# Two edits in a staged attention kernel: a two-slot gate on weight conversions, and a third key tile joined on POOL

## The chip, the cores and the metric

One Trainium2 chip, one core. The metric is the device time of one launch in microseconds, median of three runs; lower is better.

## The reference

Three blocks follow each other. The first is attention in which a query sees only keys that share its nearest centroid; the second mixes tokens through cosine and sine of a projection; the third is a low-rank token mixer and a feed-forward layer.

```python
# q, k, v: (2, 8, 768, 64); 16 centroids for each head
mask   = q_assign[:, :, :, None] == k_assign[:, :, None, :]
scores = where(mask, scale * q @ k.T, -1e9)
attn   = exp(scores - max(scores)); attn /= sum(attn) + 1e-9
x      = attn @ v                              # -> (2, 768, 512)
theta  = x @ w_theta
y      = w_tok_r @ (x * cos(theta)) + w_tok_i @ (x * sin(theta))
u      = x + y;   u = u + relu(u @ w_ch)
h      = (u.T @ U @ V).T + u
out    = h + relu(h @ w_ch1) @ w_ch2
```

The weight inputs are float64 in memory, except q, k, v and the centroids. The kernel loads their 8-byte words and makes float32 of them on the chip.

## The kernel before

Attention runs in eight groups g (0 to 7), each one batch and two heads h. Keys are cut into six tiles kt of 128. P, the exponentials of the scores, is kept transposed: `pt[g, h, kt]` has keys on partitions and 768 queries on the free axis. A group is walked in six slots p (0 to 5). In one slot TensorE makes the scores of two key tiles of one head (`scores_pair`, L304; ACT takes the exponentials, L309) and the plain maxima of the next group's scores (`max_pair`, L251; VectorE reduces them, L255). `max_split` (L271 and L272, POOL) splits the maxima in two bf16 parts after slots 2 and 5, and `max_rows` (L282, L285) puts them as rows into the packed queries. PSUM is a ring of eight banks, given out in order.

In slot 5 of groups 1 to 6 TensorE then multiplies P with v (`pv`, L317) and adds up P over the keys with a matrix of ones (`sum_keys`, L346): one round of four matmuls (8 records in the trace) for each key tile that is handed to it. `join_keys` (L332) adds key tiles 0 and 1 of a head beforehand, in slots 1 and 4, on POOL in groups 0 to 3 and on VectorE after that, so five rounds are left. VectorE transposes the result (L349); in slot 2 of the following group `row_sums` (L358, L359, then eight small copies on POOL, L365) takes the reciprocal, and in slot 5 `spread` (L371) and `norm_x` (L375) scale the group's x.

Splitting and packing of group g + 2 happens in slots 0 and 1 (`split_hi` L188 on ACT, `split_lo` L193 on POOL, then 16 transfers by `pack` through L213), masks of group g + 2 in slot 2 or 3 (`mask_rows`, ACT and 8 transfers through L213). SyncE issues all transfers, in order.

Conversions of weights fill gaps. A `Convert` loads its tile into one of three staging buffers (`load`, L390), then ACT takes the high words (`magnitude`, L399), VectorE shifts the low words (`low`, L402) and joins both (`join`, L406); then ACT rounds a high part (`wh`, L411) and POOL subtracts it (`wl`, L415). Each call of `conv_step` does one of these: `magnitude` (unless done before), `low`, nothing, then a last step that joins, puts the following tile's `magnitude` on ACT, and issues the next load. `wh` and `wl` of a finished tile come at the next slot's start, or at the end of a group. While attention runs, `held[0]` is true.

Which work falls into a slot is counted out by `fill(t)`: the slot's allowance t is added to a debt `owed`, and items are taken until it is not above zero, first from the list `bg` (the cluster assignment of a later group, L128 to L152, `spread`, `norm_x`, each with a price), then conversion steps at 1.0. The allowance is 0.3 in most slots, 9.6 in slot 5 (4.8 in groups 0 and 1). Weights come in the order wth 0 to 2 (queued at group 1), wr 0, wi 0, wr 1, wi 1, wr 2, wi 2 (group 2), and the other six, `late`, at group 6.

The mixer follows (`theta` L534, `ymix` L576 and so on); it asks for each converted tile by `conv_until`.

Of the kernel before, what the change touches and what calls it, by code (L numbers as in the profile page):

```python
# [16 lines left out]
ALU = mybir.AluOpType  # L17
# [8 lines left out]
NT = S // P  # L26
# [15 lines left out]
def tile_cluster_block(ctx: ExitStack, tc: tile.TileContext, qk, v, cent, wth, wr, wi, wch,  # L42
                       u_in, v_in, w1, w2, cst, out):
    nc = tc.nc
# [7 lines left out]
    def slot(name, dt=F32, shape=None):  # L52
        return sp.tile(shape or [P, S], dt, tag="slot", name=name)
# [5 lines left out]
    def bank(name, keep=None):  # L59
        i = ring.popleft()  # L60
        if keep is None:
            ring.append(i)
        else:
            kept.setdefault(keep, []).append(i)
        return pp.tile([P, 512], F32, tag=f"bank{i}", name=name)
# [46 lines left out]
    def cols(hf):  # L112
        return slice(hf * HALF, (hf + 1) * HALF)
# [174 lines left out]
    pt, v_t, pvt, xT = {}, {}, {}, {}  # L288
# [24 lines left out]
    def pv(g, kt, hf):  # L313
        if kt == 0 and hf == 0:
            pvt[g] = banks("pv", "pv")
        for r in range(0, P, 32):
            nc.tensor.matmul(out=pvt[g][hf][r:r + 32, :HALF], lhsT=v_t[g][:, kt, r:r + 32],  # L317
                             rhs=pt[g, r // 64, kt][:, cols(hf)],
                             start=(kt == 0), stop=(kt == NT - 1))
# [7 lines left out]
    rl, lsum, joined = {}, {}, {}  # L327

    def join_keys(g, h, eng):
# [2 lines left out]
        eng.tensor_tensor(t, pt[g, h, 0], pt[g, h, 1], op=ALU.add)  # L332
        joined[g, h] = t

    def sum_keys(g, a, n=3):

        ps = bank("l")
        x = [[pt[g, h, kt] for kt in range(3 * a, 3 * a + n)] for h in range(2)]
        if (g, 1) in joined and a == 0:
            x = [[joined.pop((g, h)), *x[h][2:]] for h in range(2)]  # L340
        n = len(x[0])
        for i in range(n):
            for h in range(2):
                for hf in range(2):
                    o = 32 * (2 * h + hf)
                    nc.tensor.matmul(out=ps[o:o + 32, :HALF], lhsT=ones, rhs=x[h][i][:, cols(hf)],  # L346
                                     start=(i == 0), stop=(i == n - 1))
        lt = slot("lt")[:, :HALF]
        nc.vector.transpose(lt, ps[:, :HALF])  # L349
        lsum[g, a] = lt  # L350
# [67 lines left out]

    conv_load, conv_in, conv_do, conv_after = deque(), deque(), deque(), deque()
    held = [False]  # L420

    def conv_start():
        while conv_load and len(conv_in) < STAGED:
            c = conv_load.popleft()
            c.load()
            conv_in.append(c)

    def conv_step(n=1):

        for _ in range(n):  # L430
            if conv_after and not held[0]:
                conv_after.popleft()()
            if not conv_do:
                conv_start()
                if not conv_in:
                    return
                c = conv_in[0]

                def last(c=c):
                    c.join()  # L440
                    conv_in.popleft()
                    conv_after.extend([lambda f=f: f(c) for f in c.done])
                    if conv_in:
                        conv_in[0].magnitude()
                    conv_start()

                conv_do.extend((c.low, lambda: None, last))
                if c.t is None:
                    conv_do.appendleft(c.magnitude)
            conv_do.popleft()()  # L450
# [6 lines left out]
    def weigh_in(src, n, dst):  # L457
        return [Convert(src, n, i, keep_split(dst)) for i in range((n + S - 1) // S)]
# [384 lines left out]
    def attention():  # L843


        ORDER = [(0, 0), (0, 2), (0, 4), (1, 0), (1, 2), (1, 4)]
        BURST = (2, 5)
        pvq = deque()
        held[0] = True

        def next_pv():
            g, kt, hf = pvq.popleft()
            pv(g, kt, hf)
            if kt == NT - 1 and hf:
                pv_out(g)

        for g in range(NG):
            nxt = g + 1 < NG
            if g == 1:
                conv_load.extend(weigh_in(wth, NP * DM, wth_t))  # L860
                conv_start()
            if nxt:
                load_v(g + 1)
            if g < 2:
                bg.extend(assign.pop(g + 2))
            if g + 3 < NG:
                for i in range(2):
                    load_raw(g + 3, i)
            if g == 2:
                tok = [c for p in zip(weigh_in(wr, NT * S, wr_t), weigh_in(wi, NT * S, wi_t)) for c in p]  # L870
                conv_load.extend(tok[:6])
                conv_start()
                late = tok[6:]
            if g == 6:
                conv_load.extend(late)
                conv_start()
            if not nxt:
                for t in range(NP):
                    bg.append((1., lambda t=t: split_x(0, t, nc.gpsimd)))
            order = [(1, 0), None, (1, 2), None, (1, 4), None] if g == 0 else ORDER  # L880
            for p in range(NT):
                ready = len(pvq)
                if order[p]:
                    h, a = order[p]
                    scores_pair(g, h, a)
                    if h:
                        pvq.extend((g, kt, hf) for kt in (a, a + 1) for hf in range(2))
                if g == 0 and p < 2:
                    mask_direct(1, p, nc.scalar if p else nc.vector)
                if nxt:  # L890
                    max_pair(g + 1, p // 3, 2 * p % 6)
                    if p % 3 == 2:
                        max_join(g + 1, p // 3)

                while conv_after:
                    conv_after.popleft()()
                if p in ((1, 4) if g < 4 or not nxt else (2, 4)):
                    join_keys(g, p // 4, nc.gpsimd if g < 4 else nc.vector)
                    if 4 <= g < NG - 1 and p == 4:
                        owed[0] -= .95  # L900
                if p < 2 and g + 2 < NG:
                    split_half(g + 2, p)
                if p == (3 if g < 2 else 2) and g + 2 < NG:
                    mask_rows(g + 2)
                long = 0 < g < NG - 1 and p == 5
                if long:
                    if g + 3 < NG:
                        (_, sims), *items = assign_items(g + 3)
                        sims()
                        bg.extend(items)  # L910
                    max_rows(g + 1, 0)
                if g > 0 and p == 5:
                    bg.appendleft((.95, lambda: norm_x(g - 1)))
                    bg.appendleft((.97, lambda: spread(g - 1)))
                fill(2.5 if not nxt else .3 if p not in BURST or (g > 1 and p == 2) else 9.6 if g > 1 else 4.8)
                if not nxt:
                    for _ in range(min(ready, (2, 2, 2, 0, 4, 4)[p])):
                        next_pv()
                    if p == 5:
                        sum_keys(g, 0)  # L920
                elif long:
                    ready = len(pvq) - (6 if g == NG - 2 else 0)
                    for n in range(ready):
                        if n == ready // 2:
                            max_rows(g + 1, 1)
                        next_pv()
                    sum_keys(g, 0, NT)
                elif p == 2 and g < 2:
                    if g > 0:
                        max_rows(g, 1)  # L930
                        sum_keys(g - 1, 1)
                    for _ in range(min(ready, 6)):
                        next_pv()
                elif p == 5:
                    max_rows(g + 1, 0)
                    for _ in range(min(ready, 6)):
                        next_pv()
                    sum_keys(g, 0)
                    (_, sims), *assign[g + 3] = assign_items(g + 3)
                    sims()  # L940
                if g > 0 and p == 2:
                    row_sums(g - 1)
            while bg:
                fill(.5)
            while g and conv_after:
                conv_after.popleft()()
        held[0] = False
        while len(pvq) > 1:
            next_pv()
        nc.scalar.activation(out=warm, in_=warm, func=AF.Sin)  # L950
        next_pv()
        sum_keys(NG - 1, 1)
# [286 lines left out]
```

## Time and profile before

| what | value |
|---|---|
| median of three runs | 675.95 us (675.38, 675.95, 677.36) |
| profiled execution, its own time | 675.26 us |
| its span | 673.5 us |
| mean granted clock of TensorE | 0.997 of full speed |
| TensorE busy | 658.3 us, 98% |
| VectorE (DVE) busy | 462.3 us, 69% |
| ScalarE (ACT) busy | 358.3 us, 53% |
| GpSimd (POOL) busy | 313.1 us, 46% |

The span is the time from the first to the last instruction in the profile; 1.8 us of the execution's time lie around it. Times in the rows below are microseconds from the span's start. Attention takes the stretch up to 231 us, the mixer and the two later blocks the rest.

### The profile page before, as it was taken

What the parts mean: (1) busy time and instruction counts of PE and PEld (TensorE: products, weight loads), DVE (VectorE), ACT (ScalarE), POOL (GpSimd) and SP (SyncE); (2) the same over time, 40 slices, a digit from 0 to 9 for tenths busy, and PEclk for the clock granted to TensorE, in tenths of its full rate; (3) what the DMA queues carried; (4) which work ended last, traced back from release to release, by engine and by line L of the source; (5) the groups of instructions that cost most, each with busy time, mean ns of one, the idle gap of its engine ahead of it and who ended that gap; (6) DMA issues with size and microseconds to landing.
All of it is one profiled execution on the core that took longest, in us unless ns stands there. A gap on an engine that the chain in (4) does not pass through costs nothing.

```text
span 673.5 us, 11931 instructions
## 1 busy us (share of the span) xinstructions
PE 658.3 (98%) x4559; PEld 579.8 (86%) x4560; DVE 462.3 (69%) x795; ACT 358.3 (53%) x726; POOL 313.1 (46%) x325
## 2 busy tenths in 40 slices
PE   8899999999889999999999999999999999999998
PEld 3567777777565599999999998899999999999997
DVE  7888698797688575547375547758876576776554
ACT  8648477667388554455464445634553444543231
POOL 9445156324048532114233144967666564746221
PEclk9899999999999999999999999999999999999999
DMA  6868668766604211003101221012221222110013
GB/s 201 216 146 261 173 143 254 218 165 172 219 0 150 87 48 33 1 0 110 48 24 33 77 65 48 26 38 80 73 84 35 76 79 79 32 32 2 0 48 141
DMA packets 21786, 62.57 MB, mean 93 GB/s; under 512 B 4224, under 2 KB 7296, under 8 KB 21728
## 3 DMA queue, kind: packets, MB, share of 16 engines
q1 hardware_dynamic: 21728, 61.80, 31.7%
q8 instruction: 36, 0.59, 0.4%
q14 instruction: 22, 0.18, 0.1%
HBM read 40.35 MB, written 3.15 MB: 65 GB/s over the span
## 4 chain that ended last, share of the span: by engine, by line
PE 89%; DVE 6%; ACT 2%; DMA 1%; SPq 1%; issue 1%; POOL 0%; POOLq 0%; DVEq 0%; ACTq 0%
PE acc L810 17%; PE q L758 15%; PE y L576 15%; PE st L304 8%; PE pv L317 8%; PE h L596 5%; PE th L534 5%; PE smax L251 3%; DVE mx L255 3%; PE l L346 3%; PE g L712 3%; PE acc L731 2%; DMA st<-in_wi_dram 1%; PE sims L121 1%; PE tp L614 1%; SPq L213 1%
## 5 line engine op out<-in xcount | busy, mean ns | idle before, releaser
L810 PE MATMUL acc<-g,wh 128*128 128x384 f32 x448 | 113.6, 334 | 0.0
L772 POOL TENSOR_TENSOR g<-sum,g 128x384 fp32r<-128x384 f32 x56 | 61.9, 1107 | 83.4 <-ACT g L771 83.4
L255 DVE TENSOR_REDUCE mx<-smax 128x1 f32<-128x512 f32 x144 | 89.1, 680 | 14.5 <-PE smax L251 14.5
L766 DVE TENSOR_TENSOR xT<-acc,xT 128x384 f32<-128x384 f32 x112 | 61.9, 555 | 46.3 <-PE acc L810 46.2
L309 ACT ACTIVATE p<-st 128x512 f32<-128x512 f32 x192 | 80.2, 530 | 25.1 <-PE st L304 24.6
L576 PE MATMUL y<-wh,z 128*128 128x384 f32 x384 | 87.6, 340 | 0.3 <-ACT z L554 0.3
L304 PE MATMUL st<-qp,kp 128*128 128x256 f32 (+1 forms) x384 | 79.4, 348 | 2.4 <-ACT p L309 1.5
L810 PEld LDWEIGHTS acc<-g,wh 128*128 128x128 f32 x448 | 80.7, 188 | 0.1
L415 POOL TENSOR_TENSOR wl<-cv,wh 128x768 fp32r<-128x768 f32 (+1 forms) x31 | 56.2, 1819 | 49.2 <-ACT wh L411 35.4
L810 PE MATMUL acc<-g,wl 128*128 128x384 f32 x224 | 74.8, 334 | 0.0
L304 PEld LDWEIGHTS st<-qp,kp 128*128 128x128 f32 x384 | 57.8, 191 | 19.5 <-issue 7.2
L770 ACT ACTIVATE sum<-sum 128x384 f32<-128x384 f32 x56 | 29.3, 523 | 82.3 <-DVE sum L766 82.3
L766 DVE TENSOR_TENSOR sum<-q,sum 128x384 f32<-128x384 f32 x98 | 53.0, 553 | 24.3 <-PE q L758 20.8
L576 PEld LDWEIGHTS y<-wh,z 128*128 128x128 f32 x384 | 66.9, 188 | 0.5 <-ACT z L554 0.5
L317 PE MATMUL pv<-p,v 128*32 128x384 f32 x768 | 66.6, 487 | 0.0
L560 POOL TENSOR_TENSOR z<-tht,z 128x256 fp32r<-128x256 f32 x24 | 18.2, 756 | 91.7 <-ACT z L554 91.6
L317 PEld LDWEIGHTS pv<-p,v 128*32 128x32 f32 x768 | 38.9, 110 | 18.7 <-issue 8.2
L406 DVE SCALAR_TENSOR_TENSOR cv<-cv,st 128x768 int32<-128x768 int32 (+3 forms) x47 | 49.5, 1054 | 0.8
L251 PE MATMUL smax<-kp,qp 128*128 128x512 f32 x192 | 44.6, 349 | 4.6 <-ACT qp L285 2.0
L576 PE MATMUL y<-wl,z 128*128 128x384 f32 x192 | 48.8, 335 | 0.0
L251 PEld LDWEIGHTS smax<-kp,qp 128*128 128x128 f32 x192 | 32.8, 191 | 15.3 <-issue 4.3
L193 POOL TENSOR_TENSOR lo<-raw,hi 128x768 fp32r<-128x768 f32 x16 | 29.3, 1838 | 35.4 <-ACT hi L188 24.2
(177 smaller groups left out, 1440.8 us busy)
## 6 DMA issues: line engine op xcount, KB each, us to landing
st<-in_w_dram SPq DMA_DIRECT2D x17, 512.0 KB, 3.6
st<-in_w_dram SPq DMA_DIRECT2D x10, 768.0 KB, 4.2
raw<-in_qk_dram SPq DMA_DIRECT2D x16, 384.0 KB, 5.0
qp<-hi SPq DMA_DIRECT2D x26, 192.0 KB, 3.1
st<-in_wr_dram SPq DMA_DIRECT2D x6, 768.0 KB, 4.3
st<-in_wi_dram SPq DMA_DIRECT2D x6, 768.0 KB, 5.8
kp<-hi SPq DMA_DIRECT2D x32, 96.0 KB, 3.1
qp<-lo SPq DMA_DIRECT2D x32, 96.0 KB, 2.7
```

What stands on the lines that cost most here:

```text
L251: nc.tensor.matmul(out=ps[:, c:c + w], lhsT=qp[s, h, 0][:, (a + j) * P:(a + j + 1) * P], rhs=kp[s, h, 0][:, k0:k0 + w], start=True, stop=True)
L255: nc.vector.tensor_reduce(mx_t[g, h][:, o:o + n], ps.rearrange("p (n w) -> p n w", n=n), axis=AX.X, op=ALU.max)
L304: nc.tensor.matmul(out=ps[:, c:c + n], lhsT=kp[s, h, w][:, (a + j) * P:(a + j + 1) * P], rhs=qp[s, h, w][:, q0:q0 + n], start=(w == 0), st ...
L309: nc.scalar.activation(out=pt[g, h, a + j][:, q0:q0 + n], in_=ps[:, c:c + n], func=AF.Exp, scale=float(D) ** -0.5)
L317: nc.tensor.matmul(out=pvt[g][hf][r:r + 32, :HALF], lhsT=v_t[g][:, kt, r:r + 32], rhs=pt[g, r // 64, kt][:, cols(hf)], start=(kt == 0), st ...
L406: nc.vector.scalar_tensor_tensor(t, t, 3, self.lw, op0=ALU.logical_shift_left, op1=ALU.bitwise_or)
L415: nc.gpsimd.tensor_tensor(t[:, :c.w], c.t, f32(c.hi[:, :c.w]), op=ALU.subtract)
L576: nc.tensor.matmul(out=yps[u, j][hf][:, :HALF], lhsT=lhs, rhs=w[st][e][:, hf * HALF:(hf + 1) * HALF], start=(st == 0 and n == 0), stop=(st ...
L758: nc.tensor.matmul(out=ps[:, :HALF], lhsT=w[a][:, j * P:(j + 1) * P], rhs=u_block(self.b, y, e, j), start=(n == 0), stop=(n == 5))
L766: nc.vector.tensor_tensor(out, ps[:, :HALF], x, op=ALU.add)
L772: nc.gpsimd.tensor_tensor(t[:, 1], r, f32(t[:, 0]), op=ALU.subtract)
L810: nc.tensor.matmul(out=ps[:, :HALF], lhsT=wv[a], rhs=self.g[i, hf][:, x], start=(m == 0), stop=(m == 5))
```

## The change

A conversion gets a gate for the time in which attention holds: `load` notes a clock that counts slots, and `magnitude` of a tile may start only once the clock is two ahead of its load. Where it may not, `conv_step` returns without doing anything, and the step's price is still paid. `late` is queued at group 5 instead of 6. In groups 1 to 3 a new `join_third` on POOL adds key tile 2 of P in place onto the sum of tiles 0 and 1, for head 0 in slot 2 and for head 1 in slot 5; `sum_keys` then skips that tile and has four rounds.

```diff
+    wide = set()
+    def join_third(g, h):
+        t = joined[g, h]
+        nc.gpsimd.tensor_tensor(t, t, pt[g, h, 2], op=ALU.add)
+        wide.add(g)
     def sum_keys(g, a, n=3):
...
-            x = [[joined.pop((g, h)), *x[h][2:]] for h in range(2)]
+            x = [[joined.pop((g, h)), *x[h][3 if g in wide else 2:]] for h in range(2)]
...
+    clock = [0]
+    def landed(c):
+        return not held[0] or clock[0] - c.at > 1
     def conv_start():
         while conv_load and len(conv_in) < STAGED:
             c = conv_load.popleft()
             c.load()
+            c.at = clock[0]
             conv_in.append(c)
...
-                if not conv_in:
+                if not conv_in or not (conv_in[0].t is not None or landed(conv_in[0])):
                     return
...
-                    if conv_in:
+                    if conv_in and landed(conv_in[0]):
                         conv_in[0].magnitude()
...
-            if g == 6:
+            if g == 5:
                 conv_load.extend(late)
                 conv_start()
...
             for p in range(NT):
                 ready = len(pvq)
+                clock[0] = NT * g + p
...
+                if 0 < g < 4 and p in (2, 5):
+                    join_third(g, p // 5)
```

In slot 5 the new line stands after `max_pair`, `max_join` and the `wh` and `wl` of a finished conversion, and before `max_rows`, `fill`, `pv` and `sum_keys`; in slot 2 before `mask_rows`, `fill` and `row_sums`.

## Rows read from the trace of the kernel before

**Rows 1.** The page: engines' busy time; the chain that ended last, by engine and line.
```profile
PE 658.3 (98%) x4559; PEld 579.8 (86%) x4560; DVE 462.3 (69%) x795; ACT 358.3 (53%) x726; POOL 313.1 (46%) x325
...
PE 89%; DVE 6%; ACT 2%; DMA 1%; SPq 1%; issue 1%; POOL 0%; POOLq 0%; DVEq 0%; ACTq 0%
PE acc L810 17%; PE q L758 15%; PE y L576 15%; PE st L304 8%; PE pv L317 8%; PE h L596 5%; PE th L534 5%; PE smax L251 3%; DVE mx L255 3%; PE l L346 3%; PE g L712 3%; PE acc L731 2%; DMA st<-in_wi_dram 1%; PE sims L121 1%; PE tp L614 1%; SPq L213 1%
```

**Rows 2.** The chain in order of time, groups 5 and 6: start, duration, what.
```profile
169.35 0.97 ACT cv L399
...
175.63 5.49 DMA st<-in_wi_dram
```

**Rows 3.** ACT in order of time: start, duration, instruction; in brackets idle time before.
```profile
157.94 1.66 ACT L309 ACTIVATE p<-st 128x512 f32<-128x512 f32 x4
...
181.21 0.89 ACT L399 ACTIVATE cv<-st 128x768 f32<-128x768 f32 x1 [10.07 <-DMA st<-in_wi_dram]
...
183.87 2.31 ACT L411 ACTIVATE wh<-cv 128x768 fp32r<-128x768 f32 x3
```

**Rows 4.** ACT's waits over the span: in total, times, longest.
```profile
ACT cv L399 <- DMA st<-in_wi_dram: 10.1, 1, 10.1
```

**Rows 5.** TensorE in order of time, group 6: the instructions behind its gaps.
```profile
183.14 1.01 PE L251 MATMUL smax<-kp,qp 128*128 128x256 f32 x3 [1.98 <-ACT qp L285]
...
186.72 0.73 PE L304 MATMUL st<-qp,kp 128*128 128x512 f32 x2 [1.48 <-ACT p L309]
...
200.99 0.27 PE L282 MATMUL mrow<-identb,m 128*2 128x128 bf16 x3 [1.26 <-POOL m L272]
```

**Rows 6.** Stretches of six slots, groups 4, 5, 6: length, busy time by engine.
```profile
129.45:143.80 14.35, 14.22 (x89) 11.38 (x93) 12.58 (x23) 11.65 (x27) 7.47 (x13) 1.00 0.98 300
155.01:168.19 13.18, 13.18 (x82) 11.07 (x86) 11.43 (x21) 11.60 (x27) 6.27 (x12) 1.00 0.68 177
179.28:197.62 18.34, 14.77 (x82) 11.11 (x84) 12.31 (x22) 14.47 (x32) 7.99 (x13) 1.00 0.28 112
```

**Rows 7.** SyncE's issues in order of time: the last mask transfer, the load behind it.
```profile
174.95 0.59 SPq L213 DMA_DIRECT2D kp<-oh  x1
175.63 0.53 SPq L390 DMA_DIRECT2D st<-in_wi_dram  x1
```

**Rows 8.** Line 390, all its loads: time from issue to landing.
```profile
DMA to landing us min/median/max: 2.3/4.1/8.9
```

**Rows 9.** The chain in order of time: the row sums of group 2.
```profile
100.94 3.23 PE l L346 x40
```

**Rows 10.** Three lines over the span: count, shortest, median, longest in ns.
```profile
L332 POOL TENSOR_TENSOR pj<-p,p x8: 1834/1848/2017, 35.7 to 115.7; 128x768 f32<-128x768 f32 x8
...
L132 DVE TENSOR_TENSOR eqw<-s_t,mxc x8: 557/558/878, 8.2 to 148.6; 128x384 bf16<-128x384 f32 x8
...
L147 DVE TENSOR_TENSOR eqw<-eqw,mi x8: 517/557/559, 9.8 to 150.1; 128x384 bf16<-128x384 bf16 x8
```

**Rows 11.** POOL in order of time, groups 1 and 2.
```profile
59.71 0.32 POOL L272 TENSOR_TENSOR m<-mx,m 128x6 bf16<-128x6 f32 x1
...
90.26 1.86 POOL L332 TENSOR_TENSOR pj<-p,p 128x768 f32<-128x768 f32 x1
...
95.50 1.83 POOL L415 TENSOR_TENSOR wl<-cv,wh 128x768 fp32r<-128x768 f32 x1
```

**Rows 12.** VectorE in order of time, groups 1 to 3.
```profile
60.59 0.56 DVE L147 TENSOR_TENSOR eqw<-eqw,mi 128x384 bf16<-128x384 bf16 x1
...
88.23 3.61 DVE L255 TENSOR_REDUCE mx<-smax 128x1 f32<-128x512 f32 x6
...
107.85 1.67 DVE L402 TENSOR_SCALAR st<-st 128x512 int32<-128x512 int32 x1
```

**Rows 13.** The chain in order of time, group 1, slot 3.
```profile
62.75 0.50 PE smax L251
```

**Rows 14.** VectorE in order of time, end of group 2.
```profile
104.22 0.58 DVE L349 STREAM_TRANSPOSE lt<-l 128x384 f32<-128x384 f32 x1 [1.31 <-PE l L346]
```

## Prediction

> **What bounds the kernel now.** I read the page's totals and its chain first: TensorE is busy for 98% of the 673.5 us span and its lines carry 89% of the chain [rows 1]. A gain therefore has to come out of TensorE's own work or out of one of its few gaps. The chain names only one transfer inside the run, `st<-in_wi_dram`, at 1% [rows 1]; so I followed the chain in order of time around it. At 169.35 ACT runs a conversion's first pass (`magnitude`, L399), at 175.63 begins a 5.49 us transfer, and at 181.21 ACT runs L399 again [rows 2, 3]. ACT's own list says why: before that instruction it stood 10.07 us idle, waiting for the transfer [rows 3]. It is ACT's only wait for a load in front of L399 in the whole run [rows 4].
>
> ACT's queue is in order, so everything behind the waiting instruction is late: the rows of maxima, xT, three `wh` passes from 183.87 on, and only then the exponentials of group 6 [rows 3]. TensorE pays 1.98 us and 1.48 us in two gaps [rows 5], but that is not the whole price. The six slots of group 5, from their first score to the maxima's rows, take 13.18 us, the same six of group 6 take 18.34 us [rows 6]. Group 6 has no splits, packs or masks of a later group, so 13.18 us is a fair length for it, and the stall costs 5.16 us, 1.7 us of them as slots that wait for late exponentials and late maxima on VectorE.
>
> Why the data is late: SyncE sends 16 pack transfers and 8 mask transfers, about 0.6 us each, before it reaches the load of `wi` 2 at 175.63 [rows 7], while the code asks for `magnitude` of that tile in the same slot in which it asks for the load.
>
> **The change, part by part.**
>
> *The gate.* I walked the steps of `fill` by hand. In slot 5 of group 5 the debt is -1.03 + 9.6 = 8.57; `spread` and `norm_x` take 1.92, which leaves seven conversion steps. The first finishes `wr` 1 and issues the load of `wi` 2; the seventh finishes `wr` 2 and, before, put `magnitude` of `wi` 2 on ACT. With the gate the load carries clock 35, so the pass is not allowed before clock 37, slot 1 of group 6. There the debt is -0.35 + 0.3 + 0.3 = 0.25, one step, and `magnitude` takes it, behind the exponentials of that slot. Group 5's slot 1 finished its exponentials at 159.60 [rows 3], 4.6 us after the group began; 179.28 + 4.6 = 183.9, and somewhat less without the `hi` pass that stands between in group 5. The load of `wi` 2 landed at 181.12 [rows 2]. Loads of this line take 4.1 us at the median and 8.9 us at most [rows 8], so the worst would be 184.5, 0.6 to 1.5 us of wait on ACT. I take no wait, and 1.5 us as the upper end. ACT was busy for 11.60 of the 13.18 us of group 5's slots, with two `hi` passes and a mask among them [rows 6]; in group 6 one pass stands in their place.
>
> What the gate moves besides: `low` of `wi` 2 goes from slot 1 to slot 5 of group 6, onto VectorE behind `norm_x` (in front of the transpose of the row sums, where TensorE does not wait for it). In group 7 the conversions run one step later; the kernel enters the mixer with one step more to do on `wi` 5, which is read seven iterations later. Everywhere else the walk gives the same steps in the same slots, since every other load is older than two slots when its turn comes.
>
> *The load issued earlier.* With `late` queued at group 5, the loads of `wr` 3 and `wi` 3 go to SyncE directly behind `wi` 2 and ahead of v of group 7, instead of behind it. All still stand behind the 24 pack and mask transfers, that v is read only in group 7, and the four loads move the same bytes: nothing for the path.
>
> *So the stall:* -5.16 us. The lower end is the bare gaps, -3.46 us. The 1.26 us gap at 200.99 [rows 5] stays: VectorE and POOL reach the maxima's split as late after the slots as before.
>
> *Row sums in four rounds.* One group's row sums are 40 matmul records in 3.23 us [rows 9], five rounds of 8 records, 0.646 us a round. They stand alone on TensorE. Three groups lose one round each: -1.94 us. This term is TensorE work, and its ends are close.
>
> *The six adds on POOL.* One such add takes 1.85 us at the median [rows 10]; six are 11.1 us on an engine that is busy 46% of the span [rows 1]. What waits for each: in slot 2, behind it on POOL, the eight copies of `row_sums`, then the add of head 1 and the maxima's split; in slot 5 only `wl` of a conversion and TensorE's row sums. In group 2, the tightest, POOL is through `wl` at 97.3 [rows 11], VectorE's `norm_x` then has its turn, the add ends near 100.0, and the row sums began at 100.94 [rows 9]: 0.9 us spare.
>
> The cost is on VectorE. Where POOL adds or subtracts from SBUF, VectorE's instructions with two SBUF inputs are held: `eq` (L132) took 878 ns at its longest, where a POOL subtraction overlapped it, against 557 ns at the least [rows 10], while six L255 reductions from 88.23 on took their usual 0.6 us each although POOL's add of 90.26 ran beside the last of them [rows 11, 12]. The Trainium skill (SBUF — State Buffer, Who interferes with whom) states it as a lock: of a VectorE instruction with two SBUF inputs and a GpSimd one that reads SBUF, the later waits for the whole of the other, and a reduction never does; by it L147 below is held, and the sum stands as it is, while without it the sum would be 668.2.
>
> Group 1, slot 2: POOL finishes the split at 60.03 [rows 11], so the add runs from 60.05 to 61.9. VectorE reaches `onehot` (L147, two SBUF inputs) at 60.59 [rows 12]; it would start at 61.9, 1.3 us late. That line is on the chain, and TensorE's maxima wait for what follows it (62.75) [rows 13]: **+1.3 us**. L147 itself overlapped no POOL add before (517 to 559 ns, [rows 10]), so the ends are 0 and 1.85.
> Groups 2 and 3, slot 2: VectorE is in reductions; about 0. The adds in slot 5 hold `norm_x` and the masks' steps for 0.9 to 1.4 us, but VectorE then idles before the transpose of the row sums, least of the three groups in group 2, 1.31 us [rows 14]. Group 2 is the edge: its last `wh` comes about 1 us later and meets the exponentials of group 3. In group 3 a `low` pass that now takes 1.67 us beside a POOL subtraction [rows 12] may fall into a free place instead. I take 0 for both, with -0.7 and +0.9 as ends.
>
> **Sum.** The profiled execution took 675.26 us, the median of three runs is 675.95. 675.26 - 5.16 - 1.94 + 1.3 = **669.5 us**. That run lies at the fast end of the three (675.38 to 677.36), so a median may come out up to 0.7 us higher. Nothing later gives it back: the chain holds no other transfer that reaches 1% [rows 1].
>
> **The rivals.**
> *The stall leaves only its bare gaps* because group 6 is then paced by VectorE, as group 4 (14.35 us, [rows 6]) was more than group 5, or the load lands late: 675.26 - 3.46 - 1.94 + 1.3 = 671.2. Against it: group 5 had more on ACT and POOL and ran in 13.18. 15%.
> *The adds are free*, L147 slips in ahead of the add in group 1, and group 3's held `low` comes free: 675.26 - 5.16 - 1.94 - 0.7 = 667.5. 15%.
> *The gate does not do what it says*: the load comes so late that ACT is caught again in group 6 for as long. 675.26 - 1.94 + 1.3 = 674.6, no measurable change. It needs a landing near 191, where 175.63 and the longest flight give 184.5 [rows 7, 8]. 5%.
> *Slower: POOL's adds hold VectorE, and VectorE holds TensorE through the score and maximum banks.* Price at most 6 x 1.85 = 11.1 us: 675.26 - 7.10 + 11.1 = 679.3. It ends above the kernel before from the point where more than 7.1 of the 11.1 us reach TensorE. For it: group 1's chain runs through just such instructions. Against: the idle time of [rows 14] behind the three adds of slot 5, and the reductions that are not held. 4%.
>
> **How the numbers follow.** The forecast keeps 61%. A measurement of this kernel can tell about 0.3%, 2.0 us, from no change, so faster means below 673.9: forecast, bare gaps and free adds, 0.90; within, 0.06; slower, 0.04. The range takes in 667.5 and 671.2, the ends of the adds in groups 1 to 3 and the 0.7 us between the profiled run and the median: 666.8 to 672.8.
>
> **What would show it.** Right: no wait of ACT for a load in front of L399; L399 once in slot 1 of group 6; its six slots within 13 to 13.5 us; row sums of groups 1 to 3 with 32 records in 2.58 us; L147 near 1.9 us in group 1 and the slots of that group longer by about 1.3 us; the 1.26 us gap of group 6 still there. Wrong: an ACT wait for `wi` 2 or `wi` 3 in group 6; slots of group 6 above 14.5 us; TensorE waiting for the added POOL line in front of the row sums; new gaps in the first slots of group 3.

## The result

The changed kernel takes 670.31 us (median of six runs, 669.57 to 673.77) against 676.83 us for the kernel before in the six runs that go with them (675.38 to 678.64). The ratio is 0.9911, with a 95% interval of 0.9884 to 0.9937, so 4.3 to 7.9 us were won. The profiled execution took 670.76 us, of which the span is 669.0.

First the page of the changed kernel, as in [rows 1]: engines' busy time and the chain that ended last. Lines after 332 have new numbers: `magnitude` is L407, `low` L410, `join` L414, `sum_keys` L354, `norm_x` L383, and the added POOL line is L340.

```profile
PE 656.9 (98%) x4535; PEld 579.6 (87%) x4536; DVE 463.8 (69%) x795; ACT 359.1 (54%) x726; POOL 325.7 (49%) x331
...
PE 91%; DVE 5%; POOL 1%; ACT 1%; issue 0%; DMA 0%; SPq 0%; POOLq 0%; DVEq 0%
```

The 1% of the chain that was a transfer is gone, POOL is busy for 12.6 us more, TensorE has 24 records less. ACT in order of time, from the end of group 5 on, answers to [rows 3]:

```profile
177.22 2.30 ACT L419 ACTIVATE wh<-cv 128x768 fp32r<-128x768 f32 x3
180.72 1.64 ACT L309 ACTIVATE p<-st 128x512 f32<-128x512 f32 x4 [1.20 <-PE st L304]
182.81 1.64 ACT L309 ACTIVATE p<-st 128x512 f32<-128x512 f32 x4 [0.45 <-PE st L304]
184.31 0.91 ACT L407 ACTIVATE cv<-st 128x768 f32<-128x768 f32 x1
185.08 1.68 ACT L309 ACTIVATE p<-st 128x512 f32<-128x512 f32 x4
```

The three `wh` passes now end before group 6's exponentials are wanted, and `magnitude` of `wi` 2 stands behind the exponentials of slot 1, without idle time before it.

To see where the time went, both kernels are cut at the first score of each group. The stretches of the kernel before (columns: stretch, its length, then busy time of TensorE, its weight loads, VectorE, ACT, POOL with instruction counts, granted clock, share of the DMA engines, GB/s); prologue with group 0, groups 1 to 7, and the rest:

```profile
0.00:50.50 50.50, 44.28 (x286) 25.58 (x287) 39.78 (x89) 33.48 (x64) 32.50 (x40) 0.97 0.71 188
50.50:79.36 28.86, 28.78 (x277) 21.29 (x275) 21.09 (x39) 17.12 (x38) 10.00 (x16) 1.00 0.77 213
79.36:104.10 24.74, 24.74 (x230) 19.28 (x229) 22.27 (x37) 17.50 (x37) 11.46 (x18) 1.00 0.65 165
104.10:129.38 25.28, 25.18 (x230) 19.22 (x229) 21.07 (x36) 17.67 (x37) 13.41 (x19) 1.00 0.77 206
129.38:154.94 25.56, 25.43 (x230) 19.27 (x229) 21.20 (x37) 16.29 (x35) 9.70 (x16) 1.00 0.73 215
154.94:179.28 24.34, 24.34 (x222) 18.01 (x221) 19.52 (x32) 14.36 (x31) 6.73 (x15) 1.00 0.64 166
179.28:206.42 27.14, 22.31 (x174) 15.29 (x172) 20.86 (x32) 19.81 (x40) 10.74 (x17) 1.00 0.27 102
206.42:231.38 24.96, 24.96 (x235) 12.43 (x233) 18.20 (x15) 20.01 (x40) 20.55 (x16) 1.00 0.41 131
231.38:673.50 442.12, 438.27 (x2696) 429.46 (x2692) 278.31 (x480) 202.11 (x404) 197.95 (x172) 1.00 0.16 50
```

The same stretches of the changed kernel:

```profile
0.00:51.68 51.68, 46.06 (x285) 26.50 (x287) 39.61 (x89) 33.71 (x64) 32.50 (x40) 0.93 0.70 184
51.68:81.00 29.32, 28.16 (x268) 20.88 (x266) 22.61 (x39) 17.15 (x38) 13.54 (x18) 1.00 0.73 204
81.00:105.12 24.12, 24.12 (x221) 18.89 (x220) 22.81 (x37) 16.67 (x36) 16.33 (x19) 1.00 0.66 161
105.12:130.05 24.93, 24.79 (x221) 18.85 (x220) 22.25 (x37) 18.46 (x38) 16.50 (x20) 1.00 0.80 220
130.05:155.57 25.52, 25.42 (x229) 19.27 (x229) 21.19 (x37) 16.33 (x36) 10.62 (x17) 1.00 0.81 218
155.57:179.94 24.37, 24.37 (x222) 18.05 (x221) 19.52 (x32) 18.50 (x38) 8.55 (x17) 1.00 0.63 161
179.94:201.95 22.01, 20.75 (x175) 15.29 (x173) 19.89 (x32) 15.89 (x33) 8.36 (x16) 1.00 0.32 119
201.95:226.88 24.93, 24.93 (x234) 12.44 (x232) 17.24 (x15) 20.17 (x40) 21.04 (x17) 1.00 0.42 142
226.88:669.00 442.12, 438.26 (x2696) 429.46 (x2692) 278.68 (x480) 202.19 (x404) 198.23 (x172) 1.00 0.16 50
```

Group 6 loses 5.13 us (27.14 to 22.01). Group 1 is 0.46 longer, group 2 is 0.62 and group 3 is 0.35 shorter, groups 4, 5 and 7 stay within 0.04, and the 442.12 us after attention are the same to the hundredth: nothing is given back later. From group 1 on the changed kernel is 5.68 us shorter. The two spans differ by 4.5 only, because the stretch before group 1, which the change does not touch, took 1.18 us longer in this one execution, at a granted clock of 0.93 against 0.97. In the ten profiles of this study, all with the same code there, that stretch took 50.5 to 52.2 us; so the experiments are read by the groups, not by the spans.

### The profile page after: what moved, and what is told of

The parts are those of the page before. It is cut to its first block, busy times and chain, and to the rows that moved or that the text cites. A ratio compares the mean times of both kernels' runs of the same rounds, so it can differ in the third digit from the quotient of the medians.

```text
span 669.0 us, 11891 instructions
## 1 busy us (share of the span) xinstructions
PE 656.9 (98%) x4535; PEld 579.6 (87%) x4536; DVE 463.8 (69%) x795; ACT 359.1 (54%) x726; POOL 325.7 (49%) x331
## 4 chain that ended last, share of the span: by engine, by line
PE 91%; DVE 5%; POOL 1%; ACT 1%; issue 0%; DMA 0%; SPq 0%; POOLq 0%; DVEq 0%
PE acc L824 17%; PE q L772 15%; PE y L590 15%; PE st L304 9%; PE pv L317 9%; PE h L610 5%; PE th L548 5%; PE smax L251 4%; PE l L354 3%; DVE mx L255 3%; PE g L726 3%; PE acc L745 3%; PE tp L628 1%; PE th L552 1%; PE sims L121 1%; PE h L672 0%
## 5 line engine op out<-in xcount | busy, mean ns | idle before, releaser
L414 DVE SCALAR_TENSOR_TENSOR cv<-cv,st 128x768 int32<-128x768 int32 (+3 forms) x47 | 49.3, 1049 | 0.8
```

The costliest lines, as they stand in the source:

```text
L414: nc.vector.scalar_tensor_tensor(t, t, 3, self.lw, op0=ALU.logical_shift_left, op1=ALU.bitwise_or)
```

## The experiments

My theory has two parts. The gate alone takes ACT's wait for the load away, and that wait was the whole of group 6's excess. The adds save 0.65 us of row sums in each of three groups, and the one in slot 2 of group 1 gives 1.1 us back, because it holds a VectorE instruction that TensorE's maxima wait for. The rivals: only the bare gaps come back; it was the earlier queueing of `late`; the adds are free, or cost time wherever they stand; VectorE and POOL wait for each other through semaphores only, and no instruction is held while it runs.

**The gate without the adds.**

```diff
-                if 0 < g < 4 and p in (2, 5):
-                    join_third(g, p // 5)
```

> The gate and the earlier queueing of `late` stay, the six adds of key tile 2 are taken out (five rounds of row sums again). My theory: the wait of ACT in front of L399 alone made group 6 long, so group 6 (first score to the next group's first score) takes 22.0 us instead of 27.2, no wait for a load in front of L399, and groups 1 to 3 take their old 28.9, 24.7 and 25.3 us; in all 5.2 us below the kernel before. Rival 1, only the bare gaps come back: group 6 takes 23.7, 3.5 us in all. Rival 2, part of group 6's gain came from the adds further up: group 6 stays above 23.

Ratio to the kernel before 0.9896 (0.9883 to 0.9909). Groups 1, 2, 3 and 6:

```profile
50.73:79.61 28.88, 28.82 (x276) 21.31 (x274) 21.09 (x39) 17.10 (x38) 9.98 (x16) 1.00 0.78 215
79.61:104.35 24.74, 24.74 (x229) 19.28 (x228) 22.23 (x37) 17.50 (x37) 11.46 (x18) 1.00 0.66 168
104.35:129.63 25.28, 25.18 (x230) 19.22 (x229) 21.04 (x36) 17.63 (x37) 13.35 (x19) 1.00 0.72 196
...
179.52:201.52 22.00, 20.74 (x174) 15.27 (x172) 19.87 (x32) 15.89 (x33) 8.35 (x16) 1.00 0.31 114
```

Group 6 takes 22.00 with the gate alone, and groups 1 to 3 their old lengths. Both rivals are out: more than the bare gaps came back (23.7 would have been those), and none of it comes from the adds. In the times of the runs the adds cannot be told from nothing: without them the ratio is 0.9896, with them 0.9911, and their intervals overlap. What the adds are worth is read from the groups alone: from group 1 to the mixer 175.73 us here, 175.20 in the changed kernel.

**The adds without the gate.**

```diff
-        return not held[0] or clock[0] - c.at > 1
+        return True
...
-            if g == 5:
+            if g == 6:
                 conv_load.extend(late)
```

> Only the six adds, the gate taken out and `late` queued at group 6 again. My theory: each of groups 1 to 3 loses 0.65 us of row sums, group 1 pays 1.1 us back because POOL's add holds L147, group 3 pays 0.3 back at a held `low`; groups 1 to 3 take 29.3, 24.1 and 24.9, group 6 keeps its 10 us wait on ACT and its 27.2; in all 0.5 us below the kernel before, which the times can hardly tell from none. Rival, the adds cost nothing on VectorE: 1.9 us below, group 1 at 28.2. Rival, POOL's adds hold VectorE everywhere: groups 1 to 3 each longer than before.

Ratio 0.9982 (0.9972 to 0.9993). Groups 1, 2 and 3 took 29.32, 24.12 and 24.89 us, as expected; group 6 took 26.72, with ACT's wait at 9.7 us instead of 10.07, so it was 0.4 us shorter than I had said. By the groups the adds bring 1.0 us here, 0.4 of it in group 6 with that shorter wait; why the wait was shorter was not tried.

**No gate, but `late` at group 5, and the adds.**

```diff
-        return not held[0] or clock[0] - c.at > 1
+        return True
```

> The changed kernel without the gate: `late` at group 5 and the adds kept. My theory: ACT is caught in front of L399 for 9.5 to 11 us again, since the pass still stands in the slot of its load; group 6 takes 26.7 to 27.5, and in all the kernel stands about 0.5 us below the one before. Rival, the earlier queueing is what takes the stall away: group 6 at 22.0. Rival, without the gate `wr` 3, now loaded in the same slot, catches ACT a second time: group 6 longer than 28.

Ratio 0.9983 (0.9964 to 1.0002). ACT in order of time, group 6:

```profile
180.66 0.89 ACT L407 ACTIVATE cv<-st 128x768 f32<-128x768 f32 x1 [10.01 <-DMA st<-in_wi_dram]
```

The wait is back at 10.01 us, and group 6 takes 27.11. The earlier queueing does not remove the stall.

**The gate, but `late` at group 6 again.**

```diff
-            if g == 5:
+            if g == 6:
                 conv_load.extend(late)
```

> The changed kernel with `late` queued at group 6 again, the gate and the adds kept. My theory: the gate alone takes the wait off ACT, the earlier queueing only swaps the order of three loads behind the masks; group 6 takes 22.0, no wait for a load in front of L399, the time is that of the changed kernel within 0.3 us by the trace. Rival: the loads of `wr` 3 and `wi` 3 come too late without it and ACT or the conversions of group 7 wait; group 6 or 7 longer by over 0.5 us.

Ratio 0.9902 (0.9873 to 0.9931). Group 6 took 22.00 us and group 7 24.94, against 22.01 and 24.93 in the changed kernel. That edit is worth nothing here; the gate does all.

**Head 0's add in slot 3.**

```diff
-                if 0 < g < 4 and p in (2, 5):
+                if 0 < g < 4 and p in (3, 5):
                     join_third(g, p // 5)
```

> The changed kernel, but head 0's add stands in slot 3 instead of slot 2, behind the reciprocals' copies on POOL. My theory: L147 of group 1 is not held any more (0.56 us instead of 1.64), the gap of 1.16 us in front of TensorE's maxima in group 1 goes back to none, group 1 takes 28.2 instead of 29.3, groups 2 and 3 stay at 24.1 and 24.9; 1.1 us below the changed kernel. Rival, the add costs its time wherever it stands in POOL's queue: it delays head 1's add and the maxima's split, TensorE waits in front of `max_rows` or of the row sums, and group 1 is no shorter than 29.

Ratio 0.9888 (0.9875 to 0.9901). VectorE in group 1, and the length of that group:

```profile
60.62 0.56 DVE L147 TENSOR_TENSOR eqw<-eqw,mi 128x384 bf16<-128x384 bf16 x1
```

```profile
50.54:78.75 28.21, 28.17 (x269) 20.88 (x267) 21.50 (x39) 17.15 (x38) 13.53 (x18) 1.00 0.77 213
```

L147 is back at 0.56 us, TensorE has no gap of over 0.1 us in the group, and the group takes 28.21 instead of 29.32: 1.11 us, the price that the place of one add had. The add itself still runs, behind the copies of the reciprocals, and delays nothing that TensorE waits for; the rival falls. Group 3 took 24.76, 0.17 less than in the changed kernel.

**One more add behind head 0's, in group 1.**

```diff
+                if g == 1 and p == 2:
+                    nc.gpsimd.tensor_tensor(slot("again"), pt[g, 0, 0], pt[g, 0, 1], op=ALU.add)
```

> The changed kernel with one more POOL add of the same size behind head 0's add in slot 2 of group 1, into a tile that nobody reads. My theory (VectorE instructions that use both operands' or double read paths from SBUF wait for the whole of a POOL add): the first add holds L147 as before (1.64 us); the second begins at L147's end and holds `low` (L410), 0.52 us before, to about 1.8; group 1 takes 30.5 instead of 29.3. Rival, VectorE and POOL only queue behind each other through semaphores (the copies of the reciprocals come later): the second add delays only the copies, and group 1 stays at 29.3.

Ratio 0.9936 (0.9924 to 0.9948). Group 1 took 31.93 us, 2.61 more than in the changed kernel, where I had expected 1.2 more. VectorE and POOL in order of time:

```profile
61.12 1.65 DVE L147 TENSOR_TENSOR eqw<-eqw,mi 128x384 bf16<-128x384 bf16 x1
62.81 0.58 DVE L152 STREAM_TRANSPOSE eqw<-eqw 128x384 bf16<-128x384 bf16 x1
63.31 1.56 DVE L410 TENSOR_SCALAR st<-st 128x768 int32<-128x768 int32 x1
```

```profile
60.52 1.84 POOL L340 TENSOR_TENSOR pj<-pj,p 128x768 f32<-128x768 f32 x1
62.32 2.13 POOL L919 TENSOR_TENSOR again<-p,p 128x768 f32<-128x768 f32 x1
```

The first add holds L147 as before. The second, whose result nobody reads and which nobody waits for by a semaphore, holds `low` from 0.52 to 1.56 us: TensorE's gap in front of the maxima grows from 1.16 to 2.20, by the same 1.04. So it is not a matter of semaphores, and the rival falls. The Trainium skill (SBUF — State Buffer, Who interferes with whom) counts both among those that can contend with a GpSimd instruction, the one for its two SBUF inputs, the other as a `tensor_scalar`, which can enter a two-port mode. The two rows agree; in which mode `low` ran, no row shows.

The other 1.57 us came after the gap. Granted clock in stretches around and behind TensorE's gap (it is the third column from the right):

```profile
61.10:65.42 4.32, 2.12 (x14) 1.71 (x12) 4.23 (x5) 2.82 (x6) 3.35 (x2) 1.00 1.04 287
65.42:68.99 3.57, 3.57 (x14) 3.05 (x15) 2.74 (x7) 1.85 (x4) 2.71 (x9) 0.65 0.91 209
68.99:72.29 3.30, 3.30 (x22) 2.32 (x23) 2.30 (x5) 1.65 (x4) 0.59 (x1) 0.86 0.96 222
```

Behind the 2.20 us gap TensorE was granted 0.65 and 0.86 of its full clock, a mix of its two levels (1.2 and 2.4 GHz), for about 7 us; before that it had stood idle for those 2.20 us; the eight records of scores in slot 4 lasted 2.16 us instead of 1.57. In the changed kernel, behind a gap of 1.16 us, the same stretch was at 1.00. The drop need not come each time: of the five timed executions of this kernel, three had a mean granted clock of 0.992 and took 672.66 to 673.11 us, the profiled one among them; one had 0.995 (671.48) and one 1.000 (671.44), and at 1.000 no such drop can have happened.

**A gate of one slot.**

```diff
-        return not held[0] or clock[0] - c.at > 1
+        return not held[0] or clock[0] - c.at > 0
```

This stands on the kernel with head 0's add in slot 3.

> The kernel with head 0's add in slot 3, and a gate of one slot instead of two. My theory: in slot 0 of group 6 the debt leaves no conversion step, so the pass of `wi` 2 falls into slot 1 with either gate; group 6 takes 22.0, no wait in front of L399, the same time as with two slots; in group 7 one conversion step comes a slot earlier and changes nothing for TensorE. Rival, two slots are needed: ACT waits for the load in group 6, which takes over 22.5.

Ratio 0.9886 (0.9855 to 0.9916). Group 6 took 21.99 us, with no wait for a load in front of L407, and `magnitude` stood 4.35 us behind the group's first score, against 4.37 in the changed kernel. One slot would do here; the walk through `fill` gives the reason, that no step is left for slot 0.

**Adds in groups 1 to 6.**

```diff
-                if 0 < g < 4 and p in (2, 5):
+                if 0 < g < NG - 1 and p in (3, 5):
                     join_third(g, p // 5)
```

> The kernel with head 0's add in slot 3, and the POOL adds in groups 4 to 6 as well, so twelve in all; a try for more. My theory: POOL is idle for most of these groups' ends, each loses another round, 0.65 us; groups 4, 5, 6 take 24.9, 23.7 and 21.4, 1.9 us below the kernel with head 0's add in slot 3. Rival: in group 6 the add in slot 5 starts only behind the maxima's split at 194 and TensorE waits for it in front of the row sums, and VectorE's normalization, held by the adds, comes late; groups 4 to 6 no shorter than 25.5, 24.4 and 22.0.

Ratio 0.9863 (0.9836 to 0.9889), median 668.32 us. Groups 4, 5 and 6:

```profile
129.24:154.11 24.87, 24.77 (x222) 18.88 (x221) 22.23 (x37) 16.49 (x36) 12.72 (x19) 1.00 0.74 211
154.11:177.87 23.76, 23.76 (x214) 17.59 (x213) 21.24 (x32) 18.05 (x38) 13.36 (x18) 1.00 0.69 179
177.87:199.35 21.48, 20.10 (x166) 14.88 (x164) 19.38 (x31) 15.44 (x33) 11.57 (x17) 1.00 0.27 107
```

Against the kernel with head 0's add in slot 3 (25.50, 24.36 and 21.98) that is 0.63, 0.60 and 0.50 us, close to a whole round each. It is below both kernels: from group 1 to the mixer 172.13 us, against 175.20 in the changed kernel and 180.88 before. By the medians it is only 0.4 us below the kernel with head 0's add in slot 3 (668.71), so the gain of these six adds too is read from the groups.

## Why the prediction was right

The forecast was 669.5 us on the level of the profiled run, 5.8 us below its 675.26; a median up to 0.7 higher was allowed for. From group 1 on, the traces show 5.68. The profiled execution took 1.26 us more than the forecast, 1.18 of it in the stretch before group 1. The median of 670.31 is 0.81 above the forecast, just over that 0.7, and inside the range of 666.8 to 672.8. That the sum came so close is in part luck: the hold in group 1 was put 0.19 too dear and group 3 0.30 too cheap, and these two partly cancel.

**The bound.** TensorE's stall in group 6 hung on one load, as [rows 2 to 5] said: the gate alone brings group 6 to 22.00, and without it ACT's wait of 10 us is there again.

**The gate, -5.16 us: measured -5.13.** The comparison of group 6 with group 5 [rows 6] was the step that carried the sum, and it held; the six slots of group 6 in the changed kernel answer to [rows 6] so:

```profile
180.01:193.10 13.09, 13.09 (x79) 10.97 (x82) 11.32 (x21) 10.56 (x25) 6.13 (x12) 1.00 0.39 162
```

13.18 was forecast. The bare gaps of [rows 5], 3.46 us, were two thirds of it; who counts only the idle time of TensorE misses the slots that ran late behind it. In the stretches of group 6 above, 1.56 us of the gain stand in TensorE's busy time (22.31 against 20.75 us, for 174 and 175 records at a granted clock of 1.00), where no gap shows them. The walk through `fill` put `magnitude` into slot 1, where ACT's row at 184.31 shows it, without a wait. The gap in front of the maxima's rows stayed, as forecast, at the 1.26 us of [rows 5]:

```profile
196.52 0.27 PE L282 MATMUL mrow<-identb,m 128*2 128x128 bf16 x3 [1.26 <-POOL m L272]
```

**`late` one group earlier, nothing: measured nothing** (22.00 and 24.94 us in groups 6 and 7 without it).

**Row sums, -1.94 us.** The chain of the changed kernel has 32 records in 2.58 us where [rows 9] had 40 in 3.23:

```profile
78.49 2.58 PE l L354 x32
```

**The hold in group 1, +1.3 us: measured +1.11.** L147's longest time was 559 ns in [rows 10], and POOL's added line and L147 now stand in order of time so:

```profile
61.18 1.83 POOL L340 TENSOR_TENSOR pj<-pj,p 128x768 f32<-128x768 f32 x1
```

```profile
61.78 1.64 DVE L147 TENSOR_TENSOR eqw<-eqw,mi 128x384 bf16<-128x384 bf16 x1
```

and on TensorE stands a gap that was not there (L357 is the transpose of the row sums, behind L147 in VectorE's order):

```profile
65.03 0.50 PE L251 MATMUL smax<-kp,qp 128*128 128x512 f32 x1 [1.16 <-DVE lt L357]
```

The place and the mechanism were as forecast. L147 lost 1.08 us where 1.3 was said: POOL's add began 0.60 us ahead of it instead of 0.54, and L147 ended 0.41 us after the add's recorded end, so it was let in some 0.15 us before that end. That it is the place of the add and nothing else, the add in slot 3 shows.

**Groups 2 and 3, 0: measured +0.03 and +0.30.** Group 2 was free although its adds did hold VectorE; the idle 1.31 us of [rows 14] covered them. Group 3 was mis-sized. I had left open whether its `low` pass [rows 12] would fall into a free place. It did not: held by the POOL subtraction of 108.70, it took longer than the 1.67 us of [rows 12]:

```profile
108.70 1.86 POOL L193 TENSOR_TENSOR lo<-raw,hi 128x768 fp32r<-128x768 f32 x1 [0.41 <-ACT hi L188]
```

```profile
108.87 1.97 DVE L410 TENSOR_SCALAR st<-st 128x512 int32<-128x512 int32 x1
```

In the kernel before, the same subtraction had begun 0.47 us ahead of `low`, and not 0.17:

```profile
107.38 1.85 POOL L193 TENSOR_TENSOR lo<-raw,hi 128x768 fp32r<-128x768 f32 x1 [1.62 <-ACT hi L188]
```

So this is an old collision that the change has only shifted, by 0.3 us inside the stated ends. What shifted it is the edge that the prediction named for group 2 and priced at 0: group 2's last `wh` pass on ACT, before and after.

```profile
103.01 0.84 ACT L411 ACTIVATE wh<-cv 128x768 fp32r<-128x768 f32 x1 [1.52 <-DVE cv L406]
```

```profile
105.52 0.84 ACT L419 ACTIVATE wh<-cv 128x768 fp32r<-128x768 f32 x1 [2.36 <-DVE cv L414]
```

It began 1.09 us ahead of group 3 before, and now begins 0.40 us after its first score; the group's first exponentials come 0.31 us later behind it, and the `hi` pass and its subtraction with them.

**The rivals.** Bare gaps only: out, by the gate alone. Adds free: out, by L147. A gate that does nothing: out. POOL's adds as the bound, 11.1 us: of their time 1.4 us reached TensorE (1.11 in group 1 and 0.30 in group 3). The chances of the three faster cases add up to 0.91, not to the 0.90 that stands there; nothing hangs on it.

## What to carry to other kernels

An engine that works in order and asks for data in the slot in which the load is issued can stall everything behind that instruction: put the request behind a condition that the load is old enough, and price the stall by comparing its stage with an equal one that has none, not by the gap on the bounding engine. Work moved to POOL is cheap in time but not in place: look at which VectorE instruction with two SBUF inputs, or which pass like `low`, will meet it, and put it beside reductions from PSUM or behind the stage's chain. An add that cost 1.1 us in one slot was free in the next.

## What the runs showed of the hardware beyond that

A VectorE instruction that is held got its turn between two POOL instructions that stood back to back. In group 2 of the changed kernel `norm_x` waited behind `wl`, and the add, already next on POOL, was shown with 2.53 us where 1.84 is usual (the second add behind L147 above, with 2.13 us, is another case):

```profile
97.01 1.82 POOL L423 TENSOR_TENSOR wl<-cv,wh 128x768 fp32r<-128x768 f32 x1
98.80 2.53 POOL L340 TENSOR_TENSOR pj<-pj,p 128x768 f32<-128x768 f32 x1
```

```profile
97.94 1.71 DVE L383 TENSOR_TENSOR xT<-xT,rb 128x768 f32<-128x768 f32 x1
```

In these rows the time for which an instruction is held stands inside its duration, on both engines, and not in the idle time in front of it; a view of waits does not show it. And in one profiled execution a gap of 2.20 us on TensorE was followed by a lower granted clock that cost another 1.57 us, while the gap of 1.16 us in the changed kernel, and those of 1.98 and 1.48 us in group 6 of the kernel before [rows 5, 6], left the granted clock of their stretches at 1.00. What tells these cases apart, these runs do not show; nor was it tried why the prologue took 50.5 us in some profiles and 52.2 in another.
